# Fused attention and two MoE layers on one core: passes over loads and weights tied behind the newest tile, v's constant columns set once, first blocks later with a buffer of their own

## The chip, the cores and the metric

The kernel runs on one core of a Trainium2 chip. The metric is the device time of one execution in microseconds; the figure that counts is the median of several runs. The engines are named as the profile names them: PE (TensorE, matmuls; PEld its weight loads), DVE (VectorE), ACT (ScalarE), POOL (GpSimd), and SP (SyncE), whose queue issues every DMA of this kernel. Each engine works through its own queue in order; an instruction whose inputs are late holds up all that stand behind it on that engine.

## The reference

Attention over pairs of averaged queries, and then two feed-forward layers one after the other:

```python
def _attn_ref(q, k, v):                      # (4, 8, 1152, 64) each
    q_pool = q.reshape(B, H, S // 2, 2, D).mean(axis=3)
    scores = 1.0 / np.sqrt(D) * np.matmul(q_pool, k.transpose(0, 1, 3, 2))
    scores = scores - np.max(scores, axis=-1, keepdims=True)
    attn = np.exp(scores)
    attn = attn / (np.sum(attn, axis=-1, keepdims=True) + 1e-09)
    return np.matmul(attn, v)

x = attn_out.transpose(0, 2, 1, 3).reshape(B * S, H * D)      # 2304 x 512
h = x @ w_in;  x = (h * np.cos(h)) @ w_out                    # layer 1, 512 -> 2048 -> 512
h = x @ w_in2; out = (h * (1.0 / (1.0 + np.exp(-h)))) @ w_out2  # layer 2, the same sizes
```

The weights of both layers come as 64-bit floats and are turned on the chip into scaled pairs of 16-bit floats (a high and a low part). The same pairs carry q, k, v, the probabilities and the layers' inputs, so most products are three matmuls.

## The kernel before, in words

The work of attention goes in 4 batches of 4 pairs of heads. A pair has 9 tiles of 128 pooled queries against all 1152 keys, 144 tiles in all. A tile t takes these steps, each on its own engine:

- scores (PE, L531 and L539) into PSUM (sp), which holds one tile;
- evacuation with the row minimum, in two parts (DVE, L550), and nb, the bias of the exponential (DVE, L555, 128x1);
- exp in place (ACT, L558), then hi, the 16-bit part of the result (ACT, L564, tile hl), then lo, what hi leaves over (POOL, L569, the other half of hl);
- a transposing DMA from hl to hlT (SP, L571), and four tiles later (LAG) the matmuls with v (PE, L582 and L586), whose sums three tiles share (group_end, DVE and ACT).

Each tile needs a slot of sc, hl and hlT; there are 4 of each. Between a tile's steps the main loop calls advance() four times, which takes one step of every generator in the list bg, and share(), which spends credit on units of layer 1. The generators are:

- pair_prep for the next pair: an absmax of each of k (two), q and v (two) (DVE, L126, tile pm), after q's two rows have been added (POOL, L456, stq), then scales, the high and low parts of q, k, v (qn, kn, vt) and two transposing DMAs (qT, kT). The tile vt of v has an extra column of ones and one of zeros behind its 64 columns, by which the probabilities' sums come out of the same matmul; they are set by two memsets (POOL, L484 and L485) for each of 32 tiles vt. When the prep is through, the pair after next is loaded (SP).
- layer1_weight_steps: 16 pieces of 1 MB of layer 1's weights, loaded on SP (wst), then three passes of VectorE over 128x1024 (L203, L207, L211), a tiny matmul (bm) for the scale, two passes of ScalarE (L224, L225) and one of GpSimd (L226).
- block_steps: two blocks of 256 rows for each batch. x_split takes the block's absmax, splits it into xn (ACT and DVE) and transposes it (xT). The tile xn takes one of the 4 slots of hl. Then the block waits X_LAG steps, if it is not of the first batch, and its units are free to go: 16 units of 12 matmuls (h, L667) and 16 of 12 matmuls (y, L722), with the cosine between.

Units are spent at RATE = 2 for each tile from the second batch on; credit that finds no unit piles up, to 4 at most. What is left of layer 1 runs after the last tile, together with the preparation of layer 2's weights and the first blocks of layer 2; then layer 2 alone.

The order on each queue is not written out: a list scheduler takes the instructions in the order in which the code traces them (a priority; "ahead" moves it), and puts one that is ready early by its own estimate ahead of others that are not. Two means bind it. pin, which is tc.keep_in_program_order, puts an instruction behind everything traced so far on its engine; the passes over the weights are pinned. tc.issue_after(ins) puts what it encloses behind one given instruction of the same engine, and leaves the rest free.

## Time and profile before

| | us |
|---|---|
| median of 3 runs (1362.78 to 1373.58) | 1365.25 |
| the profiled execution | 1363.93 |
| its span, first to last instruction | 1362.1 |
| busy: PE / DVE / ACT / POOL | 1139.0 / 1039.7 / 870.9 / 620.3 |
| first nb to the nb of the second, third, fourth batch | 29.7 to 233.7, 438.9, 628.0 |

The span falls into a short start, the 144 tiles with layer 1 beside them from the second batch on, and a second part in which only the layers are left. An engine's busy time over the whole span mixes the two, so it is read by stretches.

### The profile page before, as it was taken

Reading aid. Unit: us, or ns where it says so; the run is one execution under the profiler, and the core shown is the slowest. Engines: PE = TensorE matmul, PEld = TensorE weight load, DVE = VectorE, ACT = ScalarE, POOL = GpSimd, SP = SyncE. Lnnn points to the kernel's source line nnn. Section 1 sums busy time; section 2 is a strip of 40 time slices with the busy share of each in tenths; the row PEclk is TensorE's granted clock in tenths of the full one; section 3 lists DMA queues with packets and bytes.
Section 4 is the critical chain, followed back from the end, with each engine's and each line's share of the span. In section 5 each row is a group of like instructions: output and inputs, shape, how many; then the busy total and the mean of one; then the engine's idle time right before and its main releaser. Section 6 shows DMA issues by size and latency. Waiting matters only on the chain. (4 is left out here: it accounts for less than half of the span.)

```text
span 1362.1 us, 26442 instructions
## 1 busy us (share of the span) xinstructions
PE 1139.0 (84%) x10668; PEld 915.3 (67%) x10668; DVE 1039.7 (76%) x1927; ACT 870.9 (64%) x1061; POOL 620.3 (46%) x352
## 2 busy tenths in 40 slices
PE   2565465788988777889898899989999999999998
PEld 1343243576666556666676678778788888888887
DVE  6898888789876988888898996886757755444483
ACT  3878787778767777877788774544546633433352
POOL 1656675666556466656556562443667400000000
PEclk9667676889998889999899999999899999999999
DMA  9999999988799999988999965423444000000001
GB/s 290 202 212 226 221 231 183 163 168 166 135 204 177 201 199 198 198 151 186 157 202 188 217 129 109 106 81 71 86 91 112 32 25 32 9 16 17 17 32 32
DMA packets 509594, 186.27 MB, mean 137 GB/s; under 512 B 465952, under 2 KB 484384, under 8 KB 509472
## 3 DMA queue, kind: packets, MB, share of 16 engines
q1 hardware_dynamic: 509472, 184.59, 65.8%
q8 instruction: 83, 1.36, 0.4%
q14 instruction: 39, 0.32, 0.1%
HBM read 66.58 MB, written 9.44 MB: 56 GB/s over the span
## 5 line engine op out<-in xcount | busy, mean ns | idle before, releaser
L569 POOL TENSOR_TENSOR hl<-sc,hl 128x1152 f16<-128x1152 f32 x144 | 367.9, 2565 | 201.2 <-ACT hl L564 105.9
L531 PE MATMUL sp<-kT,qT 128*128 128x512 f16 (+1 forms) x768 | 189.4, 366 | 92.7 <-DVE sc L550 70.8
L550 DVE TENSOR_SCALAR_CACHE_REDUCE sc<-sp,psu 128x512 f32<-128x512 f32 (+1 forms) x288 | 228.9, 807 | 49.6 <-PE sp L531 46.2
L667 PEld LDWEIGHTS <-ih 128*128 128x128 f16 x2304 | 225.5, 99 | 42.9 <-issue 12.4
L558 ACT ACTIVATE sc<-sc,nb 128x1152 f32<-128x1152 f32 x144 | 179.8, 1250 | 114.4 <-DVE nb L555 77.8
L582 PE MATMUL pv<-vt,hlT 128*128 128x130 f16 (+1 forms) x1440 | 195.1, 237 | 65.9 <-DMA hlT<-hl 58.3
L582 PEld LDWEIGHTS <-hlT 128*128 128x128 f16 (+1 forms) x1440 | 146.4, 110 | 96.1 <-DMA hlT<-hl 73.4
L667 PE MATMUL h<-ys,ih 128*128 128x256 f16 x1152 | 195.5, 274 | 4.1 <-ACT gs L683 4.1
L667 PE MATMUL h<-xT,ih 128*128 128x256 f16 x1024 | 184.9, 275 | 3.2 <-DMA xT<-xn 3.1
L586 PE MATMUL pv<-vt,hlT 128*128 128x65 f16 (+1 forms) x1440 | 186.3, 207 | 0.0
L531 PEld LDWEIGHTS <-qT 128*128 128x128 f16 x768 | 76.9, 108 | 156.9 <-issue 104.2
L564 ACT ACTIVATE hl<-sc 128x1152 f16<-128x1152 f32 x144 | 164.6, 1153 | 14.5 <-DMA xT<-xn 9.7
L722 PE MATMUL y<-gh,oh 128*128 128x256 f16 x576 | 162.0, 281 | 7.1 <-ACT y L731 7.1
L722 PE MATMUL y<-gl,oh 128*128 128x256 f16 x576 | 161.8, 281 | 2.9 <-POOL gl L711 2.9
L722 PE MATMUL y<-gh,ol 128*128 128x256 f16 x576 | 161.8, 281 | 0.0
L836 PEld LDWEIGHTS <-op 128*128 128x128 f16 x1512 | 147.9, 98 | 18.0 <-issue 0.6
L667 PE MATMUL h<-ys,il 128*128 128x256 f16 x576 | 157.7, 274 | 0.0
L586 PEld LDWEIGHTS <-hlT 128*128 128x128 f16 (+1 forms) x1440 | 143.0, 108 | 15.8 <-issue 6.1
L667 PE MATMUL h<-xT,il 128*128 128x256 f16 x512 | 140.5, 274 | 0.0
L722 PEld LDWEIGHTS <-oh 128*128 128x128 f16 x1152 | 114.8, 102 | 28.1 <-issue 9.4
L711 POOL TENSOR_TENSOR gl<-tt,gh 128x1024 f16<-128x1024 f32 x36 | 92.1, 2559 | 76.4 <-DVE gh L710 71.2
L667 PEld LDWEIGHTS <-il 128*128 128x128 f16 x1152 | 113.7, 99 | 17.8 <-issue 2.9
(310 smaller groups left out, 2039.9 us busy)
## 6 DMA issues: line engine op xcount, KB each, us to landing
wst<-in_moe_w_in_dram SPq DMA_DIRECT2D x16, 1024.0 KB, 5.8
stk<-in_k_dram SPq DMA_DIRECT2D x32, 288.0 KB, 4.0
stv<-in_v_dram SPq DMA_DIRECT2D x32, 288.0 KB, 4.0
stq<-in_q_dram SPq DMA_DIRECT2D x32, 256.0 KB, 3.1
wst<-in_moe_w_out_dram SPq DMA_DIRECT2D x8, 1024.0 KB, 6.2
wst<-in_moe_w_out_dram SPq DMA_DIRECT2D x16, 512.0 KB, 6.0
ydr<-y SPq DMA_DIRECT2D x9, 512.0 KB, 4.3
y32b<-ydr SPq DMA_DIRECT2D x9, 512.0 KB, 3.3
```

The lines of the kernel that those rows point to most:

```text
L531: nc.tensor.matmul(sp[:, o - a:o - a + n], P.qT[e][:, t, :], kT[:, o:o + n], start=(e == 0), stop=(e == 1))
L550: nc.vector.tensor_scalar(out=T.sc[:, a:z], in0=sp, scalar1=T.P.su, scalar2=None, op0=ALU.mult, op1=ALU.min, accum_out=mx[:, x:x + 1],)
L558: nc.scalar.activation(out=T.sc, in_=T.sc, func=AF.Exp, scale=-1.0, bias=nb)
L564: nc.scalar.activation(out=hi, in_=T.sc, func=AF.Copy)
L569: nc.gpsimd.tensor_tensor(out=T.hl[:, 1, :], in0=T.sc, in1=T.hl[:, 0, :], op=ALU.subtract)
L582: nc.tensor.matmul(G.pv[r, T.gi], T.hlT[:, 0, c, r], P.vt[i][:, c], start=(c == 0), stop=(c == KC - 1), skip_group_check=True,)
L586: nc.tensor.matmul(G.pv[r, T.gi, 0], T.hlT[:, 1, c, r], P.vt[i][:, c, 0], start=False, stop=(c == KC - 1), skip_group_check=True,)
L667: nc.tensor.matmul(hp, wt[:, c, f * 128:(f + 1) * 128], xt(c), start=(i == 0), stop=(i == 3 * NC - 1), skip_group_check=True,)
L711: nc.gpsimd.tensor_tensor(out=G.gl, in0=t, in1=gh, op=ALU.subtract)
L722: nc.tensor.matmul(blk.y[:, oc, :], wt[:, f, oc * 128:(oc + 1) * 128], gt[:, f % 4, :], start=(f == 0 and e == 0 and oc % 2 == 0), stop=(f ...
L836: nc.tensor.matmul(bank, t[:, e, c, :], wt[:, c, :], start=start, stop=True, skip_group_check=True)
```

## The change

It has four parts.

1. pin goes. Three kinds of instruction are kept in a list as they are traced (mark): each tile's nb on DVE, its hi on ACT (where ACT makes it) and its lo on POOL. A context, behind(), puts what is traced in it behind the newest nb on DVE, the second-newest hi on ACT and the second-newest lo on POOL. The steps over the weights after the first pieces, and in pair_prep the five absmax and q's sum, are traced in it. pair_prep takes k, then q's sum, then v, then q.
2. The four buffers of vt are made once, and their columns set once, 8 memsets in place of 64.
3. X_LAG becomes 20 steps for the first batch (it was 0 there) and stays 40 for the others. xn gets a buffer of its own while attention runs, up to the last pair.
4. Credit that finds no unit is dropped.

```diff
-X_LAG = 40
+X_LAG = (20, 40)
...
+    AGE = {"dve": 0, "act": 1, "pool": 1}
...
-    pin = tc.keep_in_program_order
+    anchors = {}
+
+    @contextmanager
+    def behind():
+
+        with ExitStack() as s:
+            for kind, a in anchors.items():
+                k = AGE[kind] + 1
+                if len(a) >= k:
+                    s.enter_context(tc.issue_after(a[-k].ins))
+            yield
+
+    def mark(kind, ins):
+        anchors.setdefault(kind, []).append(ins)
...
-            sc = scale_steps(m, pspool(), (s, u), 14, True, True, True, pin)
+            sc = scale_steps(m, pspool(), (s, u), 14, True, True, True)
...
-            pin(nc.scalar.activation(out=hi, in_=t, func=AF.Copy, scale=s))
-            pin(nc.scalar.activation(out=t, in_=t, func=AF.Copy, scale=s))
-            pin(nc.gpsimd.tensor_tensor(out=lo, in0=t, in1=hi, op=ALU.subtract))
+            nc.scalar.activation(out=hi, in_=t, func=AF.Copy, scale=s)
+            nc.scalar.activation(out=t, in_=t, func=AF.Copy, scale=s)
+            nc.gpsimd.tensor_tensor(out=lo, in0=t, in1=hi, op=ALU.subtract)
...
-                g.append(piece_steps(*x, pin))
-            next(g[0])
+                g.append(piece_steps(*x, lambda ins: ins))
+            with behind():
+                next(g[0])
...
+        at.vt = []
+        for i in range(VT_BUFS):
+            vt = at.p.tile([128, KC, 2, D + 1], F16, tag="vt%d" % i, name="vt", bufs=1)
+            nc.gpsimd.memset(vt[:, :, 0, D:D + 1], 1.0)
+            nc.gpsimd.memset(vt[:, :, 1, D:D + 1], 0.0)
+            at.vt.append(vt)
...
-        nc.gpsimd.tensor_tensor(out=qs, in0=qs, in1=P.q[:, :, 1, :], op=ALU.add)
         m = small.tile([128, 5], F32, name="pm", tag="pm")
         for i in range(2):
-            absmax(m[:, 1 + i:2 + i], P.k[i], AX.XY)
-            yield
-        absmax(m[:, 0:1], qs, AX.XY)
+            with behind():
+                absmax(m[:, 1 + i:2 + i], P.k[i], AX.XY)
+            yield
+        with behind():
+            nc.gpsimd.tensor_tensor(out=qs, in0=qs, in1=P.q[:, :, 1, :], op=ALU.add)
+        for i in range(2):
+            with behind():
+                absmax(m[:, 3 + i:4 + i], P.v[i], AX.XY)
+            yield
+        with behind():
+            absmax(m[:, 0:1], qs, AX.XY)
         yield
-        for i in range(2):
-            absmax(m[:, 3 + i:4 + i], P.v[i], AX.XY)
-            yield
...
-            P.vt[i] = vt = at.p.tile([128, KC, 2, D + 1], F16, tag="vt", name="vt", bufs=VT_BUFS)
-            nc.gpsimd.memset(vt[:, :, 0, D:D + 1], 1.0)
-            nc.gpsimd.memset(vt[:, :, 1, D:D + 1], 0.0)
+            P.vt[i] = vt = at.vt[(2 * (P.b * NP + P.j) + i) % VT_BUFS]
...
-        xn = at.p.tile([128, 2, 2, DM], F16, tag="hl", name="xn", bufs=NB_H)
+        if state.xp is None:
+            xn = at.p.tile([128, 2, 2, DM], F16, tag="hl", name="xn", bufs=NB_H)
+        else:
+            xn = state.xp.tile([128, 2, 2, DM], F16, name="xn", bufs=1)
...
-            while state.credit >= 1 and next(units, False):
+            while state.credit >= 1:
+                if not next(units, False):
+                    state.credit = 0.0
+                    return
                 state.credit -= 1
...
-            if b:
-                for _ in range(X_LAG):
-                    yield
+            for _ in range(X_LAG[b > 0]):
+                yield
```

ScalarE's queue where the first two blocks meet the prep of the sixth pair, before (ps__2424 are that pair's scales; sc is exp, hl is hi; exps of two earlier tiles stand ahead of the first row):

```order
L491 ACTIVATE qn<-stq,ps__2424 128x9x64 x2
L446 ACTIVATE kn<-stk,ps__2424 128x9x64 x2
L446 ACTIVATE vt<-stv,ps__2424 128x9x64 x2
L558 ACT_TABLE_LOAD
L558 ACTIVATE sc<-sc,nb 128x1152
L683 ACTIVATE hk<-h,ca 128x512 x2
L558 ACTIVATE sc<-sc,nb 128x1152
L605 ACTIVATE x_2775<-pvs,den 128x64 x2
L702 ACT_TABLE_LOAD
L702 ACTIVATE tt<-tt,halfpi 128x1024
L649 ACTIVATE xn<-x_521,xs 128x1024
L564 ACTIVATE hl<-sc 128x1152 x3
```

The same pair's prep and the same block's xn after the change:

```order
L581 ACTIVATE sc<-sc,nb 128x1152
L514 ACTIVATE qn<-stq,ps__2351 128x9x64 x2
L467 ACTIVATE kn<-stk,ps__2351 128x9x64 x2
L467 ACTIVATE vt<-stv,ps__2351 128x9x64 x2
L587 ACTIVATE hl<-sc 128x1152
L628 ACTIVATE x_2572<-pvs,den 128x64 x2
L581 ACTIVATE sc<-sc,nb 128x1152
L675 ACTIVATE xn<-x_521,xs 128x1024
L709 ACTIVATE hk<-h,ca 128x512
L581 ACTIVATE sc<-sc,nb 128x1152
L709 ACTIVATE hk<-h,ca 128x512
L587 ACTIVATE hl<-sc 128x1152
```

Where three tiles' hi stood in a row behind four tiles' exp, each hi now stands behind its own or the next tile's exp, and the units' evacuations (hk) begin later.

GpSimd's queue around the same place, before (hl is lo, gl the low part of a unit's product, stq q's sum):

```order
L569 TENSOR_TENSOR hl<-sc,hl 128x1152 x3
L711 TENSOR_TENSOR gl<-tt,gh 128x1024
L456 TENSOR_TENSOR stq<-stq 128x9x64
L569 TENSOR_TENSOR hl<-sc,hl 128x1152 x3
L484 MEMSET vt 128x9
L485 MEMSET vt 128x9
```

And after the change:

```order
L592 TENSOR_TENSOR hl<-sc,hl 128x1152 x5
L483 TENSOR_TENSOR stq<-stq 128x9x64
L592 TENSOR_TENSOR hl<-sc,hl 128x1152 x8
L737 TENSOR_TENSOR gl<-tt,gh 128x1024
L592 TENSOR_TENSOR hl<-sc,hl 128x1152
```

The memsets are gone from between the lo passes, and q's sum has moved back among them.

VectorE's queue at the absmax of the same pair, before (pm<-stk, pm<-stv and pm<-stq are the absmax of k, v and q; den and uo belong to other work):

```order
L598 RECIPROCAL den<-den 128x3
L211 SCALAR_TENSOR_TENSOR wt<-wst,wt 128x1024
L93 TENSOR_SCALAR mw<-wm 128x1
L126 TENSOR_REDUCE pm<-stk 128x1
L126 TENSOR_REDUCE pm<-stv 128x1
L550 TENSOR_SCALAR sc,mx<-sp,psu 128x512
L550 TENSOR_SCALAR sc,mx<-sp,psu 128x640
L126 TENSOR_REDUCE pm<-stv 128x1
L111 TENSOR_SCALAR uo_78<-bm 128x1
L126 TENSOR_REDUCE pm<-stk 128x1
L126 TENSOR_REDUCE pm<-stq 128x1
```

And after the change:

```order
L578 TENSOR_SCALAR nb<-mx 128x1
L140 TENSOR_REDUCE pm<-stk 128x1 x2
L573 TENSOR_SCALAR sc,mx<-sp,psu 128x512
L573 TENSOR_SCALAR sc,mx<-sp,psu 128x640
L573 TENSOR_SCALAR sc,mx<-sp,psu 128x512
L578 TENSOR_SCALAR nb<-mx 128x1
L140 TENSOR_REDUCE pm<-stv 128x1
```

The two of k now stand right behind one tile's nb and those of v and q behind later ones, where before all five stood within one tile among the last weight passes.

## Rows read from the trace of the kernel before

**Rows 1.** Windows: the batches, the rest; busy us by engine, PEclk, DMA share, GB/s.

```profile
29.70:233.70 204.00, 115.72 (x945) 75.39 (x945) 178.65 (x395) 165.23 (x183) 129.06 (x64) 0.68 1.02 216
233.70:438.90 205.20, 171.53 (x1716) 131.20 (x1713) 168.65 (x340) 153.84 (x181) 127.44 (x67) 0.94 0.92 170
438.90:628.00 189.10, 154.12 (x1547) 115.78 (x1545) 162.70 (x334) 147.83 (x178) 112.83 (x63) 0.94 0.99 193
628.00:820.00 192.00, 173.80 (x1725) 131.73 (x1724) 171.74 (x329) 148.48 (x175) 112.59 (x58) 0.97 0.91 176
820.00:1362.10 542.10, 519.10 (x4732) 459.00 (x4730) 338.62 (x497) 245.85 (x335) 134.93 (x88) 0.98 0.21 54
```

**Rows 2.** Waits of DVE, 30 to 820 us: total us, times, longest.

```profile
DVE sc L550 <- PE sp L531: 46.2, 31, 4.1
DVE pm L126 <- DMA stk<-in_k_dram: 16.7, 11, 3.5
...
DVE pm L126 <- DMA stv<-in_v_dram: 7.0, 5, 2.3
...
DVE pm L126 <- POOL stq L456: 3.2, 2, 2.5
```

**Rows 3.** Waits of PE, 30 to 820 us.

```profile
PE pv L582 <- DMA hlT<-hl: 58.3, 30, 5.6
```

**Rows 4.** Groups of instructions, whole span, a tile's steps: busy us, mean ns, idle before.

```profile
L569 POOL TENSOR_TENSOR hl<-sc,hl 128x1152 f16<-128x1152 f32 x144 | 367.9, 2565 | 201.2 <-ACT hl L564 105.9 <-issue 45.9 <-DVE sc L550 12.1
...
L558 ACT ACTIVATE sc<-sc,nb 128x1152 f32<-128x1152 f32 x144 | 179.8, 1250 | 114.4 <-DVE nb L555 77.8 <-DVE den L598 11.7 <-DVE pm L468 6.8
...
L564 ACT ACTIVATE hl<-sc 128x1152 f16<-128x1152 f32 x144 | 164.6, 1153 | 14.5 <-DMA xT<-xn 9.7 <-DMA hlT<-hl 3.9
...
L555 DVE TENSOR_SCALAR nb<-mx 128x1 f32<-128x1 f32 x144 | 29.5, 205 | 0.9
```

**Rows 5.** DMA issues: times, median us from issue to landing.

```profile
hlT<-hl SPq DMA_TRANSPOSE x144, 4.9
```

**Rows 6.** Waits of POOL, 30 to 820 us.

```profile
POOL vt L484 <- PE pv L586: 37.3, 13, 12.0
...
POOL stq L456 <- DMA stq<-in_q_dram: 28.1, 6, 11.2
```

**Rows 7.** Groups of instructions: weight passes of layers 1 and 2, memsets.

```profile
L211 DVE SCALAR_TENSOR_TENSOR wt<-wst,wt 128x1024 int32<-128x1024 int32 x16 | 31.4, 1964 | 0.1
...
L207 DVE SCALAR_TENSOR_TENSOR wt<-wt,wst 128x1024 int32<-128x1024 int32 x16 | 28.7, 1794 | 0.2
...
L311 DVE SCALAR_TENSOR_TENSOR wst<-wst 128x1024 int32<-128x1024 int32 x16 | 20.7, 1292 | 0.0
L308 DVE SCALAR_TENSOR_TENSOR wst<-wst,wt 128x1024 int32<-128x1024 int32 x16 | 20.6, 1288 | 0.1
...
L484 POOL MEMSET vt<- 128x9 f16 x32 | 4.2, 139 | 37.6 <-PE pv L586 37.3 <-POOLq L1237 0.3
```

**Rows 8.** Windows in batch 0, columns as in rows 1.

```profile
136.00:170.00 34.00, 15.41 (x135) 10.10 (x133) 29.15 (x76) 26.72 (x32) 20.82 (x11) 0.65 1.11 221
170.00:204.00 34.00, 22.48 (x200) 16.15 (x200) 28.00 (x67) 28.30 (x29) 27.17 (x15) 0.74 1.09 231
```

**Rows 9.** Timeline of ACT: start us, us, instruction, idle before and its releaser.

```profile
255.98 1.24 ACT L558 ACTIVATE sc<-sc,nb 128x1152 f32<-128x1152 f32 x1
...
281.59 3.25 ACT L564 ACTIVATE hl<-sc 128x1152 f16<-128x1152 f32 x3
...
291.81 1.16 ACT L564 ACTIVATE hl<-sc 128x1152 f16<-128x1152 f32 x1 [4.10 <-DMA xT<-xn]
```

**Rows 10.** Timeline of SP's queue.

```profile
683.56 16.57 SPq L571 DMA_TRANSPOSE hlT<-hl  x5
```

**Rows 11.** Timeline of POOL and DVE around 456 us.

```profile
455.76 2.91 POOL L569 TENSOR_TENSOR hl<-sc,hl 128x1152 f16<-128x1152 f32 x1 [0.40 <-ACT hl L564]
...
456.37 2.33 DVE L627 TENSOR_SCALAR ca<-ui,xu 128x8 f32<-128x8 f32 x1
```

More of the change, by code (lines that the diff above doesn't have):

```diff
@@ L554, in tile_exp @@
         nb = small.tile([128, 1], F32, tag="nb", name="nb", bufs=4)
-        nc.vector.tensor_scalar(
+        mark("dve", nc.vector.tensor_scalar(
             out=nb, in0=mx[:, 0:1], scalar1=mx[:, 1:2], scalar2=PSH * math.log(2.0), op0=ALU.min, op1=ALU.add
-        )
+        ))
         nc.scalar.activation(out=T.sc, in_=T.sc, func=AF.Exp, scale=-1.0, bias=nb)
@@ L563, in tile_hi @@
         if on_act:
-            nc.scalar.activation(out=hi, in_=T.sc, func=AF.Copy)
+            mark("act", nc.scalar.activation(out=hi, in_=T.sc, func=AF.Copy))
         else:
@@ L568, in tile_lo @@
     def tile_lo(at, T):
-        nc.gpsimd.tensor_tensor(out=T.hl[:, 1, :], in0=T.sc, in1=T.hl[:, 0, :], op=ALU.subtract)
+        mark("pool", nc.gpsimd.tensor_tensor(out=T.hl[:, 1, :], in0=T.sc, in1=T.hl[:, 0, :], op=ALU.subtract))
         T.hlT = at.p.tile([128, 2, KC, 128], F16, tag="hlT", name="hlT", bufs=NB_T)
@@ L876, in attention_moe_moe_kernel @@
         state = Weights()
-        state.mp = None
+        state.mp = state.xp = None
+        xn_stack = ExitStack()
         state.ng, state.tail = 0, False
@@ L988, in block_done @@
                 state.mp = moe_pools(moe_stack)
+                state.xp = xn_stack.enter_context(tc.tile_pool(name="xn", bufs=1, reuse_waits="tile"))
             xgens[b, i] = block_steps(b, i)
@@ L1047, in attention_moe_moe_kernel @@
                 at.src_stack.close()
+                for i in range(2):
+                    finish(xgens[b - 1, i])
+                xn_stack.close()
+                state.xp = None
                 w2st_stack = ExitStack()
```

## The prediction

> **What bounds the kernel now.** I read the stretches first, then the waits engine by engine, then single places. The span has two parts [rows 1]. From 29.7 to 820 us, the attention stage, no engine is full: VectorE is the fullest with 178.65 + 168.65 + 162.70 + 171.74 = 681.7 of 790.3 us (86%); TensorE and ScalarE stand at 615 (78%), GpSimd at 482 (61%). From 820 us to the end TensorE is busy 519 of 542 us. In the second part the change alters almost nothing: after the last score matmul TensorE's order holds 9,568 instructions where it held 9,560. So the answer lies in the first part, and there in VectorE's 108.6 us of idle time: what shortens it shortens the run, since VectorE's passes are the same ones before and after.
>
> By what it waited for (30 to 820 us) [rows 2], 46.2 us of VectorE's idle time is waiting for scores, 16.7 + 7.0 = 23.7 us waiting for k and v to land ahead of their absmax, 3.2 us for q's sum. Scores come late because TensorE's queue is held up by earlier work: 58.3 us in 30 waits for a transposed probability tile (hlT) [rows 3]. hlT is the end of a chain nb, exp, hi, lo, transpose, whose bare steps take 0.2 + 1.25 + 1.15 + 2.57 + 4.9 = 10.1 us [rows 4, 5] and which has four tiles' time, 4 x 790.3/144 = 22 us, before TensorE asks for it. What eats the other 12 us is queueing: on ScalarE other passes stand between exp and hi, and on GpSimd the queue's head waits, 37.3 us in 13 waits for v's column memsets and 28.1 us in 6 waits for q's sum [rows 6].
>
> **The change part by part.**
>
> *v's columns set once.* 56 of 64 memsets go. At 139 ns [rows 7] that is 7.8 us of GpSimd, which is idle 39% of the stage: nothing by itself. With them go the 37.3 us in which a memset waited for the matmuls that still read that buffer while lo passes stood behind it. The write of v by ScalarE now meets that wait itself; it stands where it stood, up to eight tiles after the memset, and no wait of it shows in the trace; I price it at nothing (bounds 0 and 37.3 us on ScalarE, beside its 175 us of idle time in the stage).
>
> *q's sum tied and moved behind the k passes.* Before, it could stand one tile behind its own load; now in all pairs from the third on at least three tiles lie between. The 28.1 us of GpSimd's blocking should go, and 3.2 us of VectorE's waiting.
>
> *Absmax tied behind the newest nb.* This looks like the cure of the 23.7 us, but the loads move as well. Counted in tiles from the pair's second k load on SyncE's queue to its absmax on VectorE's, pairs 2 to 15: before 4, 4, 4, 4, 4, 4, 4, 4, 3, 3, 3, 4, 4, 3; now 6, 4, 2, 5, 3, 3, 5, 3, 4, 4, 4, 6, 3, 5. The mean rises from 3.7 to 4.1, but five pairs instead of four have three or fewer. I take 0. Bounds: -23.7 us if every such wait goes, and +11 us: one pair two tiles short and four one tile short of four, at 5.5 us a tile (790.3/144), make 33, against the 23.7 that are there now, plus 2 for v.
>
> *Weight pieces freed from the strict order.* Sixteen pieces, the same passes. Before, a piece's ScalarE and GpSimd passes stood behind everything written before them; now behind the second-newest tile's hi and lo, so they may fill the wait for an exp. The last piece's lo moves from the place after the 38th tile to that after the 32nd. I price the move at nothing: what is done earlier in batch 0 is missing later, VectorE stays 88% busy in batch 0, and the DMA engines show a share of 1.09 to 1.11 from 136 to 204 us, the highest of the run [rows 8], so that loads can hardly come earlier. Bounds: -13 us, which is batch 0's 204 us against its 44.1 MB at the best rate seen, 231 GB/s (191 us); and +5 us.
>
> *Work between exp and hi.* Counting ScalarE's passes between a tile's exp and its hi in the two orders, with each kind's mean from the trace, gives 2.7 us a tile before and 2.0 now (by batch 4.8, 2.8, 1.9, 1.5 and 4.5, 1.0, 1.4, 1.1). Together with GpSimd's freed (37.3 + 28.1)/144 = 0.45 us, the chain to hlT shortens by about 1.2 us a tile. The 30 waits for hlT have a mean of 1.9 us; 1.2 off each, less for the short ones, is about 30 us of TensorE's waiting. VectorE feels a part of that: it waits 46.2 us for scores where TensorE idles 175 us in the stage, 0.26. So **-8 us**; bounds 0 and -30.
>
> *First blocks later, own input buffer.* In the old order the first blocks are split and their units begin right after the last weights, beside the next pair's prep. An exp that starts at 255.98 us waits for its hi until 281.59 us, and two later ones with it, since 21 other passes, the block's xn the last of them, stand between on ScalarE; the hi after these waits another 4.10 us for a transposed xn that holds its buffer [rows 9]. In the new order xn has its own buffer, at most six passes stand between an exp and its hi there, and the first two blocks' units, which began at the 43rd tile's scores and whose last four began at the 60th, run from the 45th to the 66th. Batch 1's VectorE idle time is 205.2 - 168.65 = 36.6 us, that of batches 2 and 3 26.4 and 20.3, a mean of 23.3 [rows 1]; the excess of 13 us is this place's. I take **-10 us**; bounds 0 and -13. What it costs: the units start later, but two blocks hold 64 units and a batch of 36 tiles asks for 72, so the supply and not the start sets how many are done by the end; counted in the order, 8 of TensorE's instructions more (four matmuls) remain after the last score, at 0.28 us at most a matmul, so at most 1.1 us, and overlapped as they are **+0.4 us**. Credit that no longer piles up shifts at most four units once, which the order has already shown in that count.
>
> Sum: -8 - 10 + 0.4 = -17.6 us. The profiled execution took 1363.93 us (1.8 more than its span), so 1346.3; it lies 1.3 under the median of the three runs, and I put the median at **1347**.
>
> **The rivals.**
>
> *DMA or VectorE takes what is given (no change).* For it: share 0.91 to 1.02 over all four batches [rows 1], SyncE issues transposes back to back, five in 16.57 us [rows 10]. Against: 149 MB over the stage would take 646 us at 231 GB/s. If only q's 3 us and a part of the rest come through, 1358 to 1366, say 1362. That the ties leave VectorE's order as it was in effect would give the same time.
>
> *Slower: tied passes wait longer.* An absmax is now fixed behind an nb, and ahead of the scores' evacuation that follows it, so that a late load stops the tile. Pair 4's second k load stands only two tiles ahead. Worked out above, this costs +11 us. Its second half: kT stands four tiles ahead of its first score, now only three for pairs 5 and 13, 5.5 us each, +11. With none of the gains that is 1363.9 + 22 = 1386. It decides if a load takes more than three tile times (16 us) from its place in the queue to landing.
>
> *The shared port takes it back.* A GpSimd pass and a VectorE pass get in each other's way here: a 128x8 pass took 2.33 us beside a lo that started 0.6 us earlier [rows 11]. The two weight passes of two inputs average 1794 and 1964 ns where lo passes run all the time, against 1288 and 1292 for the like-shaped passes of layer 2 [rows 7]: (0.51 + 0.67) x 16 = 18.9 us in batch 0. If GpSimd, no longer blocked, meets twice as many of them, another 19 us are lost: 1347 + 19 = 1366. The Trainium skill, SBUF — State Buffer, "Who interferes with whom", says that the later of two such instructions "fully blocks" until the first is done; by that rule, which the 2.33 us fit, a freed GpSimd queue would give nothing back where VectorE is the bound.
>
> *Twice the gain.* If the smoother start of layer 1 and shorter chain take away half of VectorE's 108.6 us, 1364 - 54 = 1310.
>
> **How the numbers follow.** Forecast 0.45, no change 0.26, slower 0.12, port 0.05, twice the gain 0.12. A measurement of this kernel tells about 1% (13.7 us) from no change. The forecast's own spread, with the bounds of the absmax (-24, +11) and the weights (-13, +5), is about 1330 to 1362; some fifth of it lies above 1351.6. Faster by over 1%: 0.45 x 0.8 + 0.12 + 0.02 = 0.50; slower by over 1%: 0.11; the rest 0.39. The range of 8 in 10 takes in no change and the port rival and a part of the two outer ones: 1322 to 1374.
>
> **What the profile after would show.** Right: no wait of GpSimd for v's buffer, few for q; VectorE's idle time in batch 1 near 25 us; waits of TensorE for hlT near 30 us; the first score of batch 2 some 10 to 15 us earlier; from the last score to the end 550 us as before. Wrong if VectorE's waits for k and v grow past 35 us, if the busy time of its weight passes grows, or if the DMA share reaches 1.1 all over batches 1 and 2 with the tile period unchanged.

## The result, and the profile after

The changed kernel takes 1376.54 us (median of 20 runs, 1365.78 to 1386.79), the kernel before 1366.97 us in the runs made beside it (20 runs, 1362.78 to 1373.58). The ratio is 1.0061, 95% interval 1.0044 to 1.0079: slower by 0.6%, where 1347 us, 1.3% faster, had been forecast. The time lies outside the forecast range. The profiled execution of the changed kernel took 1380.47 us, 16.5 more than that of before, where the medians are 9.6 apart; so a single pair of profiles shows a few us more than the change costs.

The page after, first line of its first part. VectorE was busy for 1039.7 us before, and its number of instructions is the same, 1927: the same passes take 33.5 us longer.

```profile
PE 1142.3 (83%) x10668; PEld 915.5 (66%) x10668; DVE 1073.2 (78%) x1927; ACT 870.2 (63%) x1061; POOL 616.8 (45%) x296
```

Windows of the changed kernel, cut as in [rows 1]: the four batches and the rest; columns as there.

```profile
28.60:254.50 225.90, 117.06 (x902) 74.89 (x901) 207.65 (x406) 167.32 (x185) 136.34 (x54) 0.68 0.91 196
254.50:444.60 190.10, 164.58 (x1651) 123.32 (x1649) 169.49 (x334) 150.46 (x179) 118.13 (x48) 0.95 0.97 184
444.60:637.40 192.80, 166.22 (x1625) 123.62 (x1623) 161.19 (x328) 147.07 (x176) 114.83 (x49) 0.93 1.00 190
637.40:833.00 195.60, 168.98 (x1751) 130.19 (x1751) 184.78 (x336) 148.72 (x175) 110.71 (x47) 0.97 0.91 171
833.00:1378.70 545.70, 521.31 (x4738) 461.62 (x4737) 334.28 (x497) 246.95 (x339) 134.82 (x88) 0.98 0.21 53
```

The stage takes 225.9 + 190.1 + 192.8 + 195.6 = 804.4 us, against 790.3. VectorE's idle time in it fell from 108.6 to 81.3 us, more than the whole gain forecast (27.3 against 17.6). Its busy time rose from 681.7 to 723.1 us: +41.4, some of it passes that moved into the stage, since the rest has 4.3 less. The two make the +14.1. By batch: +21.9, -15.1, +3.7, +3.6. So batch 1 gained 15.1 us, where 10, and 13 at most, had been forecast for it from the later blocks, and batch 0 lost more than that. From the last score to the end it is 550.7 us before and 553.1 after; the repeated run of the changed kernel, below, has 547.1, so this part tells nothing.

Waits of VectorE, 28 to 833 us (total us, times, longest): the waits for k and v, 16.7 + 7.0 us in [rows 2], are 5.6 now, and that for q's sum is gone.

```profile
DVE sc L573 <- PE sp L554: 34.9, 40, 3.0
DVE sc L573 <- PE sp L562: 9.4, 5, 3.1
...
DVE pm L140 <- DMA stk<-in_k_dram: 3.8, 3, 2.1
...
DVE pm L140 <- DMA stv<-in_v_dram: 1.8, 1, 1.8
```

Waits of GpSimd in the same stretch: the waits for v's buffer and for q's load of [rows 6], 65.4 us, no longer stand in the list, but the wait of lo for hi, 105.9 us before, is 196.5 now: GpSimd waits no less, but for another engine.

```profile
POOL hl L592 <- ACT hl L587: 196.5, 51, 24.6
POOL hl L592 <- issue: 37.0, 12, 5.2
POOL gl L737 <- DVE gh L736: 28.2, 11, 6.0
```

Waits of TensorE: hlT 49.6 us, where [rows 3] has 58.3, and a single wait of 15.1 us for qT, where the only one for qT before is 6.1. The repeated run has that 15.1 again.

```profile
PE pv L605 <- DMA hlT<-hl: 49.6, 27, 10.9
PE sp L554 <- DMA qT<-qn: 16.4, 2, 15.1
PE sp L554 <- DMA kT<-kn: 5.2, 1, 5.2
```

That wait shows what happens. The timeline of the kernel before, VectorE, pair 3 (pairs counted from 0): the passes that split q and k, at their bare durations.

```profile
152.00 0.81 DVE L492 SCALAR_TENSOR_TENSOR qn<-stq,ps__1397,qn 128x576 f16<-128x576 f32 x1
...
154.32 0.81 DVE L451 SCALAR_TENSOR_TENSOR kn<-stk,ps__1397,kn 128x576 f16<-128x576 f32 x1
...
156.26 0.81 DVE L451 SCALAR_TENSOR_TENSOR kn<-stk,ps__1397,kn 128x576 f16<-128x576 f32 x1
156.98 0.32 DVE L495 COPY qn<-qn 128x576 f16<-128x576 f16 x1
```

The same pair in the timeline of the changed kernel: VectorE, GpSimd beside it, SyncE's queue, and TensorE, which waits for q.

```profile
179.93 2.63 DVE L515 SCALAR_TENSOR_TENSOR qn<-stq,ps__1391,qn 128x576 f16<-128x576 f32 x1
...
182.60 2.80 DVE L472 SCALAR_TENSOR_TENSOR kn<-stk,ps__1391,kn 128x576 f16<-128x576 f32 x1
185.33 3.39 DVE L225 SCALAR_TENSOR_TENSOR wt<-wst,wt 128x1024 int32<-128x1024 int32 x1
188.64 2.67 DVE L472 SCALAR_TENSOR_TENSOR kn<-stk,ps__1391,kn 128x576 f16<-128x576 f32 x1
...
191.30 2.41 DVE L518 COPY qn<-qn 128x576 f16<-128x576 f16 x1
...
181.90 5.74 POOL L592 TENSOR_TENSOR hl<-sc,hl 128x1152 f16<-128x1152 f32 x2
187.60 3.10 POOL L240 TENSOR_TENSOR ol<-wt,oh 128x1024 f16<-128x1024 f32 x1
190.66 2.87 POOL L592 TENSOR_TENSOR hl<-sc,hl 128x1152 f16<-128x1152 f32 x1
...
191.34 3.36 SPq L530 DMA_TRANSPOSE kT<-kn  x1
194.79 2.88 SPq L520 DMA_TRANSPOSE qT<-qn  x1
...
199.69 2.10 PE L554 MATMUL sp<-kT,qT 128*128 128x512 f16 x6 [15.05 <-DMA qT<-qn]
```

From 181.90 to 193.53 us GpSimd runs reading passes back to back, with ends at about 184.8, 187.6, 190.7 and 193.5. VectorE's next four long passes end at 185.40, 188.72, 191.31 and 193.71: each a GpSimd pass's end plus no more than its own bare duration. A split of k lasts 2.80 us instead of 0.81, the copy of q 2.41 instead of 0.32. kT's transpose is issued 0.03 us after the last split of k, and TensorE gets its scores at 199.69.

To measure this over the whole run I took, for each form of VectorE's passes (tiles, operation, shape), the tenth percentile of its durations over the traces of this study as its bare duration, and added up what every pass took above it: **VectorE's excess**. It is 182.0 us before and 213.6 us after, so it holds 31.6 of the 33.5 us; 176.6 and 208.5 us of it lie in passes that run beside a GpSimd pass. 23.2 of the 31.6 lie in batch 0 (34.0 to 57.2). There the 16 splits and copies of k and q (qn and kn) took 17.3 us before, 7.1 of them beside a GpSimd pass, and take 28.0 us now, 23.1 of them beside one: 10.7 us more. The small passes for the pairs' scales (pu, ps) take 6.8 us more, two of the weight passes (L221, L225) 4.1. A pass that waits for GpSimd counts as busy, so a part of the idle time that went may only have changed its name.

### The profile page after: what moved, and what is told of

The parts are those of the page before. It is cut to its first block, busy times and chain, and to the rows that moved or that the text cites. A ratio compares the mean times of both kernels' runs of the same rounds, so it can differ in the third digit from the quotient of the medians.

```text
span 1378.7 us, 26386 instructions
## 1 busy us (share of the span) xinstructions
PE 1142.3 (83%) x10668; PEld 915.5 (66%) x10668; DVE 1073.2 (78%) x1927; ACT 870.2 (63%) x1061; POOL 616.8 (45%) x296
## 5 line engine op out<-in xcount | busy, mean ns | idle before, releaser
L592 POOL TENSOR_TENSOR hl<-sc,hl 128x1152 f16<-128x1152 f32 x144 | 369.1, 2570 | 290.9 <-ACT hl L587 196.5
L554 PE MATMUL sp<-kT,qT 128*128 128x512 f16 (+1 forms) x768 | 194.4, 370 | 112.3 <-DVE sc L573 76.6
L605 PE MATMUL pv<-vt,hlT 128*128 128x130 f16 (+1 forms) x1440 | 195.3, 240 | 62.3 <-DMA hlT<-hl 49.6
L605 PEld LDWEIGHTS <-hlT 128*128 128x128 f16 (+1 forms) x1440 | 148.7, 112 | 92.2 <-DMA hlT<-hl 57.7
L862 PEld LDWEIGHTS <-op 128*128 128x128 f16 x1512 | 147.8, 98 | 18.4 <-issue 0.6
L609 PEld LDWEIGHTS <-hlT 128*128 128x128 f16 (+1 forms) x1440 | 144.5, 109 | 16.6 <-issue 6.9
L693 PEld LDWEIGHTS <-il 128*128 128x128 f16 x1152 | 113.9, 99 | 16.7 <-issue 1.5
```

The lines of the kernel that those rows point to most:

```text
L554: nc.tensor.matmul(sp[:, o - a:o - a + n], P.qT[e][:, t, :], kT[:, o:o + n], start=(e == 0), stop=(e == 1))
L592: mark("pool", nc.gpsimd.tensor_tensor(out=T.hl[:, 1, :], in0=T.sc, in1=T.hl[:, 0, :], op=ALU.subtract))
L605: nc.tensor.matmul(G.pv[r, T.gi], T.hlT[:, 0, c, r], P.vt[i][:, c], start=(c == 0), stop=(c == KC - 1), skip_group_check=True,)
L609: nc.tensor.matmul(G.pv[r, T.gi, 0], T.hlT[:, 1, c, r], P.vt[i][:, c, 0], start=False, stop=(c == KC - 1), skip_group_check=True,)
L693: nc.tensor.matmul(hp, wt[:, c, f * 128:(f + 1) * 128], xt(c), start=(i == 0), stop=(i == 3 * NC - 1), skip_group_check=True,)
L862: nc.tensor.matmul(bank, t[:, e, c, :], wt[:, c, :], start=start, stop=True, skip_group_check=True)
```

## The experiments

Three theories. **Port**: VectorE's passes, longer beside GpSimd's, took the gain; in its first form, a freed GpSimd does so whatever is tied. **Slack**: the tie puts q's and k's splits too late ahead of their first score (by the orders, the slack is 5, 6, 3 and 2 tiles for pairs 1 to 4 before, 1, 1, 0 and 2 now), and the tiles wait for them whatever GpSimd does. **Chain**: what helps or hurts is the length of GpSimd's step in the chain to hlT. Ratios are to the kernel before, run on the same chip, with 95% intervals; excess and batches are those of the one execution profiled.

**Parts undone and parts alone.** e_prep_free: the changed kernel with the preparation as before.

```diff
-        with behind():
-            nc.gpsimd.tensor_tensor(out=qs, in0=qs, in1=P.q[:, :, 1, :], op=ALU.add)
...
+        nc.gpsimd.tensor_tensor(out=qs, in0=qs, in1=P.q[:, :, 1, :], op=ALU.add)
```

> The changed kernel with the prep of the pairs as before: absmax and q's sum neither tied nor reordered, all else changed. Slack theory (the tie puts VectorE's last split of k and q for the next pair only 1, 1 and 0 tiles ahead of that pair's first score in batch 0, where it was 5, 6 and 3, so TensorE waits 15 us for qT): here the order gives 4, 4, 5 tiles, batch 0 comes back from 226 to about 205 us, no wait for qT or kT over 3 us after the start, and the 15 us gained in batch 1 stay: about 1355 us. Port theory (GpSimd's freed passes fall on VectorE's and lengthen them, whoever is tied): VectorE's busy time stays near 1073 us and the time at 1370 to 1380 us.

1364.33 us, 0.9965 (0.9947 to 0.9983); excess 182.3; batch 0 207.2 us. Without the tie the loss is gone, and the excess is that of before. That rules out the port theory's first form. But only 0.35% is gained, where the slack theory named about 1355 us, and the 15 us gained in batch 1 are gone too. Windows, the four batches up to the last score, columns as above:

```profile
30.24:237.41 207.17, 120.36 (x891) 74.34 (x891) 189.38 (x405) 166.93 (x186) 134.01 (x53) 0.65 0.97 207
237.41:445.45 208.04, 174.03 (x1654) 126.97 (x1653) 170.43 (x332) 149.05 (x179) 116.03 (x49) 0.94 0.92 174
445.45:631.26 185.81, 159.78 (x1641) 121.24 (x1639) 160.64 (x336) 146.70 (x175) 117.47 (x49) 0.95 1.02 196
631.26:817.46 186.20, 165.54 (x1656) 125.67 (x1656) 166.13 (x320) 143.69 (x172) 106.48 (x44) 0.95 0.92 173
```

VectorE's idle time in these is 100.6 us. Counted in the same way, from the first nb to the last score, it is 105.4 before and 80.7 in the changed kernel. So without the tie the passes stay as long as they were, but the idle time stays too.

e_prep_only: that part alone in the kernel before.

```diff
-            absmax(m[:, 1 + i:2 + i], P.k[i], AX.XY)
-            yield
+            with behind():
+                absmax(m[:, 1 + i:2 + i], P.k[i], AX.XY)
+            yield
...
```

> The kernel before with only the prep tied and reordered. The order gives slacks of 2, 1, 1, 1 tiles for pairs 1 to 4 (before 5, 6, 3, 2). Slack theory: batch 0 longer by 10 to 20 us with a wait for qT or kT of several us, about 1380 us. Port theory: weights and memsets stand as before, so VectorE's busy time stays near 1040 us and the time near 1367 us.

1366.40 us, 0.9980 (0.9954 to 1.0005); excess 191.2, batch 0 203.1 us. Alone the tie costs nothing, though it leaves pairs 1 to 4 only 2, 1, 1 and 1 tiles of slack. That speaks against slack, and the 9 us more of excess show no cost either.

e_weights_pinned: the changed kernel with the weight pieces back in the strict order.

```diff
-                g.append(piece_steps(*x, lambda ins: ins))
-            with behind():
-                next(g[0])
+                g.append(piece_steps(*x, pin))
+            next(g[0])
...
```

> The changed kernel with the weight pieces pinned as before, the prep tied, and the rest as changed. Slacks 2, 1, 1, 1. Slack theory in its narrow form (only a slack of 0 with freed weight passes between the splits costs): batch 0 at 205 us, 1360 to 1365 us. Port theory: VectorE's busy time in batch 0 back to 185 us or so, since no freed weight passes fall on lo passes: 1362 to 1368 us. If neither, and the loss is the blocks' part (1374 us by itself), 1374 us or more.

1366.11 us, 0.9999 (0.9983 to 1.0015); excess 184.8. Undoing this part, too, takes the loss away, and here batch 1 keeps its gain (188.8 us).

e_weights_only: freed, tied weights alone, the reverse of that diff in the kernel before.

> The kernel before with only the weight pieces freed and tied. Slacks 4, 4, 5, 7, then 0 for pair 5. Slack theory: batch 0 as before or better, 1360 to 1368 us. Port theory: freed weight passes meet more lo passes, VectorE's busy time in batch 0 up by 10 us or more, 1372 us or more.

1369.99 us, 1.0028 (1.0005 to 1.0050); excess 180.1, batch 0 205.7. So the tie and the freed weights raise the excess to that of the changed kernel only together. For freed weights the port theory had named 1372 us or more and 10 us more of busy time in batch 0, slack 1368 at most; neither came.

e_pace1: the changed kernel with the steps of the preparation two advances apart instead of three for pairs 1 to 4. With this pace v of the next pair is written while the last tiles two pairs back still read that buffer (pair 2's from 102.8 us, pair 0's is read until 119.5), so those tiles multiply other values; the amount of work is the same.

```diff
-PREP_PACE = (2, 2)
+PREP_PACE = (1, 2)
```

> The changed kernel with the steps of the prep two advances apart instead of three for pairs 1 to 4, the ties kept. Slacks by the order 4, 2, 2, 2 instead of 1, 1, 0, 2. Slack theory: most of batch 0's loss comes back, 1358 to 1364 us. Port theory: nothing that matters to it moves, about 1376 us.

1374.14 us, 1.0051 (1.0025 to 1.0078). The slack of pairs 1 to 4 is 4, 2, 2 and 2 tiles and the loss stays; so does the excess, 204.9. Batch 0 does come back, to 208.7 us, as slack had it, but batch 1 takes 201.1 instead of 190.1: here lateness moved time from one batch to another and did not add to it.

e_blocks_only: xn's own buffer, the later blocks and the credit's drop alone.

```diff
-X_LAG = 40
+X_LAG = (20, 40)
...
+            xn = state.xp.tile([128, 2, 2, DM], F16, name="xn", bufs=1)
```

> The kernel before with only the blocks' part: own buffer for xn, 20 steps of lag for the first batch, credit dropped. Slacks in batch 0 as before (5, 6, 3). Slack theory, which takes batch 1's 15 us as this part's gain: batch 1 at about 190 us, batch 0 at 204 us, 1352 us in all. Port theory: a denser GpSimd queue gives the gain back on VectorE, 1362 to 1370 us.

1374.11 us, 1.0029 (1.0007 to 1.0051); batch 1 218.9 us, excess 180.7 (profiled in its slowest execution, 1379.82 us). The part that was to bring 10 us in batch 1 brings nothing there by itself. No theory had this: it is above all the ranges, without more excess.

after_again: the changed kernel itself, once more on another chip.

> The changed kernel itself once more, for how far one profiled execution stands for the others: time 1366 to 1387 us. Both theories: VectorE's busy time goes with the time of the execution profiled (1040 us at 1364, 1073 at 1380), a fast one near 1055 us.

1376.95 us, 1.0068 (1.0031 to 1.0104); excess 211.9; TensorE's 15.1 us wait for qT at the same place.

**GpSimd's reading made short.** In s_before and s_after lo is formed on 288 of its 1152 columns and the rest is set to zero: three quarters of lo are left out.

```diff
-        nc.gpsimd.tensor_tensor(out=T.hl[:, 1, :], in0=T.sc, in1=T.hl[:, 0, :], op=ALU.subtract)
+        nc.gpsimd.memset(T.hl[:, 1, 288:S], 0.0)
+        nc.gpsimd.tensor_tensor(out=T.hl[:, 1, 0:288], in0=T.sc[:, 0:288], in1=T.hl[:, 0, 0:288], op=ALU.subtract)
```

> The kernel before with lo computed on the first 288 of 1152 columns alone; the other columns are set to zero by a memset, so they leave lo out. GpSimd's reading passes over the probabilities become a quarter as long. Slacks by the order 5, 6, 2, 4. Port theory (a GpSimd pass that runs beside VectorE's lengthens them): VectorE's busy time falls by 60 us or more, the run by 20 to 60 us. Slack theory: a shorter chain alone, 10 to 20 us.

> The changed kernel with the same cut: lo on 288 of 1152 columns, the others zero. Slacks by the order 2, 1, 0, 1, as short as in the changed kernel. Port theory: with the long GpSimd passes gone nothing is taken back, so it is faster than the kernel before with the same cut, by 10 to 20 us. Slack theory: the scores of pairs 2 and 3 wait for their transposes as before the cut, batch 0 is longer than in the cut kernel before by 10 to 20 us, and the whole run slower than it by 5 us or more.

1340.72 us, 0.9802 (0.9775 to 0.9828), and 1318.47 us, 0.9647 (0.9619 to 0.9675). Excess 91.2 and 92.2. With GpSimd out of the way the change is worth 1340.72 - 1318.47 = 22.2 us, where the sum of the prediction was 17.6. Windows of s_before, the four batches:

```profile
30.24:221.54 191.30, 111.45 (x924) 69.68 (x923) 152.42 (x384) 158.23 (x177) 90.16 (x95) 0.71 1.09 228
221.54:429.91 208.37, 171.59 (x1715) 131.98 (x1716) 154.59 (x352) 157.96 (x185) 91.19 (x105) 0.93 0.91 169
429.91:623.43 193.52, 167.51 (x1593) 123.04 (x1591) 142.42 (x332) 147.73 (x178) 84.84 (x101) 0.89 1.00 191
623.43:794.98 171.55, 160.25 (x1652) 122.65 (x1650) 143.75 (x325) 143.46 (x170) 79.77 (x89) 0.98 1.01 189
```

And of s_after:

```profile
28.30:238.14 209.84, 115.96 (x892) 74.44 (x890) 168.16 (x407) 167.49 (x185) 96.72 (x86) 0.66 1.00 209
238.14:418.79 180.65, 159.53 (x1636) 121.35 (x1636) 147.46 (x331) 150.53 (x178) 82.73 (x84) 0.97 1.05 193
418.79:599.49 180.70, 160.68 (x1640) 121.88 (x1641) 139.70 (x328) 145.31 (x172) 83.11 (x85) 0.93 1.09 201
599.49:770.20 170.71, 160.39 (x1671) 123.87 (x1668) 143.26 (x326) 142.57 (x173) 75.70 (x80) 0.98 1.05 195
```

Batches 1 and 2 are 27.7 and 12.8 us shorter with the change. Batch 0 is 18.5 us longer even so; it holds 407 VectorE passes instead of 384, work that is missing later, and TensorE waits 19.9 us in it for kT and qT instead of 3.9, as slack had it, without a cost to the whole.

n_before and n_after tell port from chain: GpSimd's step is as long as with the whole lo, but it writes for most of it and reads nothing there (three quarters of lo are left out again).

```diff
-        nc.gpsimd.tensor_tensor(out=T.hl[:, 1, :], in0=T.sc, in1=T.hl[:, 0, :], op=ALU.subtract)
+        nc.gpsimd.tensor_tensor(out=T.hl[:, 1, 0:288], in0=T.sc[:, 0:288], in1=T.hl[:, 0, 0:288], op=ALU.subtract)
+        for _ in range(2):
+            nc.gpsimd.memset(T.hl[:, 1, 287:S], 0.0)
```

> The kernel before with lo on 288 columns and two memsets behind it, each 865 columns, so that GpSimd is as long at a tile as before (0.84 + 2 x 0.83 = 2.5 us) and the chain as long, but reads SBUF in a third of that time; the other columns are zero, lo is left out there. Port theory: VectorE's busy time falls as with the short lo (about 950 us), the time to 1340 to 1350 us. Chain theory (the short lo gained because GpSimd's step and queue were shorter): as the kernel before, about 1367 us.

> The changed kernel with the same long but mostly not reading GpSimd step, other columns zero. Slacks by the order 1, 1, 1, 0. Port theory: faster than the kernel before with the same step, by 10 to 20 us, near 1325 us. Chain theory: near the changed kernel's 1376 us and slower than the kernel before with the same step by 5 us or more.

1345.45 us, 0.9829 (0.9780 to 0.9878), and 1320.79 us, 0.9655 (0.9610 to 0.9700): the change is worth 24.7 us. The excess is 98.6 and 112.0 us, 13.4 more with the change, and the gain comes all the same: excess is not lost time one for one. Groups of GpSimd in n_after:

```profile
L594 POOL MEMSET hl<- 128x865 f16 x288 | 240.2, 839 | 13.2
L592 POOL TENSOR_TENSOR hl<-sc,hl 128x288 f16<-128x288 f32 x144 | 123.6, 859 | 257.7 <-ACT hl L587 257.3
```

2 x 839 + 859 = 2537 ns a tile, against 2570 ns for the whole lo. A step of the old length that reads little is as good as a short one, so the length of GpSimd's step is not it. The chain theory falls.

s_prep_free: s_after with the preparation as before (the diffs of s_after and e_prep_free together).

> The changed kernel with the preparation as before (q's sum, the five maxima and their order untied) and lo formed on 288 of the 1152 columns only, the rest set to zero; three quarters of lo are left out. Compare with s_after, 1318.5 us. If the tie costs through GpSimd's passes alone, nothing of its cost is left here: 1314 to 1325 us, batch 0 208 us or more. If the tie costs also because q and k are late for TensorE, batch 0 gets shorter than 205 us and the time is 1300 to 1313 us. If the tie is a gain by itself once GpSimd is out of the way (it takes away GpSimd's wait for q), the time is 1326 us or more.

1315.26 us, 0.9639 (0.9600 to 0.9679), against 0.9647 with the tie; batch 0 202.8 us. With the short lo the tie neither costs nor gains, where with the whole lo undoing it is worth 12.2 us. What it costs goes through GpSimd's passes; as a cost to the whole run by lateness alone, slack falls. In batch 0 the lateness is there, as the sign named for it says (below 205 us, 7.0 less than with the tie), but the later batches make up for it. GpSimd's waits for q's load are back here (25.5 us in 10 waits) and cost nothing.

**The same work in shorter reading passes.** lo in two passes of 576 columns; nothing is left out.

```diff
-        nc.gpsimd.tensor_tensor(out=T.hl[:, 1, :], in0=T.sc, in1=T.hl[:, 0, :], op=ALU.subtract)
+        for o in range(0, S, S // 2):
+            z = slice(o, o + S // 2)
+            last = nc.gpsimd.tensor_tensor(out=T.hl[:, 1, z], in0=T.sc[:, z], in1=T.hl[:, 0, z], op=ALU.subtract)
```

> The changed kernel with lo in two passes of 576 columns; nothing is left out. Port theory: a VectorE pass that meets a lo waits for half a pass at most, so VectorE's busy time falls by some 30 us and the time by 10 to 15 us, to 1362 to 1366 us, if GpSimd's second instruction (about 0.3 us a tile, from 0.84 us for 288 columns and 2.57 for 1152) is hidden. Chain theory: 0.3 us more a tile on the chain, 1376 to 1380 us.

1350.25 us, 0.9863 (0.9804 to 0.9922), 12 us below the port theory's range; excess 152.7. Two groups of h_after: half a lo takes 1470 ns, so both take 14% more of GpSimd's time than the whole, yet the weight pass that averaged 2330 ns takes 1719.

```profile
L594 POOL TENSOR_TENSOR hl<-sc,hl 128x576 f16<-128x576 f32 x288 | 416.8, 1470 | 252.9 <-issue 158.0
...
L225 DVE SCALAR_TENSOR_TENSOR wt<-wst,wt 128x1024 int32<-128x1024 int32 x16 | 27.5, 1719 | 0.0
```

> The kernel before with lo in two passes of 576 columns each; nothing is left out. If the split gains by itself, since VectorE's waiting passes get in between the halves, it is worth on this kernel what it was worth on the changed one, about 26 us: 1338 to 1352 us, and h_after (1350.3 us) has then no gain of the change in it. If the split only lets the change's gain through, this kernel stays within 1360 to 1372 us. In between (1353 to 1359 us) both are in it.

1362.38 us, 0.9984 (0.9961 to 1.0008), though the excess falls from 182.0 to 149.0 there too. Waits of GpSimd and VectorE in h_before, 30 to 825 us:

```profile
POOL stq L456 <- DMA stq<-in_q_dram: 57.8, 12, 11.5
POOL vt L484 <- PE pv L588: 20.4, 8, 5.0
...
DVE pm L126 <- DMA stk<-in_k_dram: 38.5, 17, 10.0
```

VectorE's freed time went into waits: for k's loads 38.5 us instead of 16.7, while GpSimd waits 78.2 us for q's load and v's buffer. In h_after GpSimd has none of these two waits, and VectorE waits 19.8 us for k. So the split is no gain by itself; it lets the change's gain through. That the waits are why it is none by itself is read from these lines, not tried.

h_prep_free: h_after with the preparation as before.

> The changed kernel with the preparation as before and lo in two passes of 576 columns; nothing is left out. If the tie still costs with the split lo, 1332 to 1345 us, below h_after's 1350.3 by the 12 us that undoing the tie gave with lo whole. If the split has taken away what the tie cost, 1346 to 1355 us, the same as h_after. If the tie is a gain once the split has shortened GpSimd's passes, 1356 us or more.

1345.14 us, 0.9853 (0.9809 to 0.9897); excess 145.8. By the ratios it is the same as h_after within the intervals: with shorter reading passes no cost of the tie is to be seen. These two are faster than both kernels, by 1.4 to 1.5% against the one before.

**What the tie leaves unexplained.** v's columns, weights and blocks together, without the preparation's tie, against the same kernel without them: 0.4% faster with the whole lo (e_prep_free against the kernel before), 1.3% with lo in halves (h_prep_free against h_before), 1.7% with the short lo (s_prep_free against s_before). The excess hardly differs within a pair: 182.3 and 182.0, 145.8 and 149.0, 85.2 and 91.2. VectorE's idle time from the first nb to the last score falls by 4.8, 18.4 and 18.6 us. So with the lo passes whole most of the parts' gain is missing, though they take no more of VectorE's time than before. By what way was not found.

**Which part brings the 22 us.** Each part alone in s_before, by the diffs above; for v's columns:

```diff
-            P.vt[i] = vt = at.p.tile([128, KC, 2, D + 1], F16, tag="vt", name="vt", bufs=VT_BUFS)
-            nc.gpsimd.memset(vt[:, :, 0, D:D + 1], 1.0)
-            nc.gpsimd.memset(vt[:, :, 1, D:D + 1], 0.0)
+            P.vt[i] = vt = at.vt[(2 * (P.b * NP + P.j) + i) % VT_BUFS]
```

> The kernel before with the short lo and with v's columns set once, alone. The prediction priced it at nothing by itself: 1338 to 1344 us, as s_before. If the waits of GpSimd for v's buffer held up the tiles, 1325 to 1337 us.

> The kernel before with the short lo and with the weight pieces freed from the strict order and tied behind the newest tile's steps, alone. By the prediction's term for the work between exp and hi, of which this part brings most, 4 to 8 us less than s_before's 1340.7: 1332 to 1337 us. If it moves work to and fro at no gain, 1338 to 1344 us; if it costs by lateness, without GpSimd's passes, above 1344 us.

> The kernel before with the short lo (288 of 1152 columns, the rest zero; three quarters of lo are left out) and with the later blocks and xn's own buffer alone. Compare with s_before, 1340.7 us. By the prediction's term, 10 us less and all of it in batch 1: 1327 to 1334 us, batch 1 below 200 us against 208. If the gain of batch 1 comes only together with the other parts, 1337 to 1344 us and batch 1 at 205 us or more.

1342.47, 1346.01 and 1350.32 us; 0.9824 (0.9784 to 0.9863), 0.9853 (0.9788 to 0.9918) and 0.9864 (0.9817 to 0.9912), against s_before's 0.9802. None gains alone; the last two are above the ranges named for no gain, though their intervals overlap that of s_before. Freed weights move work into batch 0 (206.4 us instead of 191.3) and out of batches 1 and 2 (198.4 and 188.1 instead of 208.4 and 193.5), with nothing left over; the later blocks take batch 1 to 201.4 us, but batch 3 and the rest come out 7.2 and 6.6 us longer, the latter no more than the 6 us by which the rest differs between two executions of the changed kernel. All three together are s_prep_free, 0.9639. The gain belongs to a combination; which of them it needs was not tried.

## Why the prediction was wrong

**The step that failed** is in its first paragraph: "what shortens [VectorE's idle time] shortens the run, since VectorE's passes are the same ones before and after". The idle time did shrink, by 27.3 us. The passes are the same in number and kind, but not in length: the excess grew by 31.6 us. The sum had terms for where passes wait and none for how long they last beside GpSimd. Of the 1.9% between the forecast (1.3% faster) and the result (0.6% slower), this step accounts for 1.0: undoing the tie alone brings the excess back to 182.3 us and the time from 1.0061 to 0.9965.

**A second step failed beside it**: the terms of -8 and -10 us. In e_prep_free, where the passes are no longer than before, the kernel gains 4.8 us by the medians in place of 17.6, VectorE's idle time falls from 105.4 to 100.6 us and batch 1 takes 208.0 us. The same parts gain 1.3 and 1.7% where lo is cut in two or shortened, so what holds them back is GpSimd's long passes again; the way is open.

**The port rival** had that mechanism, at 19 us and a chance of 0.05. The price was of the right order (31.6 us of excess measured, 12.2 of time), the trigger and the passes were not. It priced the weight passes, which hold 4.1 of the 23.2 us of batch 0. And it took a GpSimd freed from blocking to be what makes passes meet; e_weights_pinned, where GpSimd waits no more for v's buffer and 2.3 us for q's load, has an excess of 184.8. What makes them meet is the order: with the preparation tied behind the newest tile's steps and the weights too, q's and k's splits come while GpSimd works through its lo passes and the weights' own. I had counted where kT's transpose stands on SyncE's queue, and not where the splits that feed it stand on VectorE's. How the two ties together bring this about was read from the orders and from pair 3, not tried pass by pass.

By the sentence of the Trainium skill (SBUF — State Buffer, "Who interferes with whom") that the later of two such instructions "fully blocks", a VectorE pass should begin its work when GpSimd's pass ends, and so end no more than its bare duration later; the timeline at 180 to 194 us shows that. The conclusion drawn from it, nothing gained where VectorE is the bound, was nearer to the result than the forecast.

**The terms.** *The sum, -17.6*: where GpSimd reads little, the change brings 22.2 and 24.7 us (s, n), so the total was about right there, but by luck, since its parts were not. *Work between exp and hi, -8, and blocks later, -10*: put in alone, the weights and the blocks bring nothing, with the whole lo (1.0028, 1.0029) or the short one; the gain of batch 1, 15.1 us, is one of parts together, with the whole lo of the tie too, and batch 0 pays for it. TensorE's waits for hlT fell by 8.7 us, not by 30. *v's columns, 0*: as forecast when alone (with the short lo). *q's sum*: the 28.1 us of blocking went, and s_prep_free, which has 25.5 us of it again, is no slower than s_after; so there they are worth nothing. *Absmax tied, 0 (-24 to +11)*: the waits for k and v fell by 18.1 us, near the good end, while VectorE's passes grew by more. *Weights freed, 0 (-13 to +5)*: within the bounds by itself, 0.3% slower, and one half of the tie's loss. *Blocks' cost, +0.4*: from the last score to the end 550.7 us before, 553.1 and 547.1 in two executions after; too small to be seen.

**The other rivals.** The slower one (a late load stops the tied absmax) did not happen: those waits are 5.6 us. Its second half, q and k too late for the scores, is there once, 15.1 us for qT at pair 3, but through the splits and not through the queue. Of the signs named as right, GpSimd's waits went and VectorE's idle time in batch 1 is 20.6 us, where about 25 was forecast; but the waits for hlT are 49.6 us and not near 30, and batch 2's first nb comes at 444.6 us instead of 438.9, later and not earlier. Of those named against it, a growing busy time of the weight passes came in part: 31.4 us in [rows 7] to 37.3 us for one kind of layer 1, though the other fell from 28.7 to 26.9. Groups of VectorE in the changed kernel:

```profile
L225 DVE SCALAR_TENSOR_TENSOR wt<-wst,wt 128x1024 int32<-128x1024 int32 x16 | 37.3, 2330 | 0.0
L221 DVE SCALAR_TENSOR_TENSOR wt<-wt,wst 128x1024 int32<-128x1024 int32 x16 | 26.9, 1683 | 0.3
...
L518 DVE COPY qn<-qn 128x576 f16<-128x576 f16 x16 | 13.2, 823 | 0.1
```

The last row, q's copy, was 5.6 us (347 ns each) before.

**What stays open**: why the three parts gain so little with the whole lo even without the tie; why weights or blocks alone cost 0.3% with no more excess; which combination of v's columns, weights and blocks brings the 22 us; and how much of the 11.5 us by which batch 0 is longer in s_prep_free than in s_before (202.8 and 191.3) is the 24 VectorE passes that moved into it.

## What to carry to other kernels

When a change only reorders work, the durations of the passes are part of what it changes: look in the profile for forms whose mean lies well above their shortest, find the engine that runs beside them, and ask of the new order which passes will now meet it. A tie that fixes a pass behind a step of the newest tile also fixes what it runs beside. Where a long reading pass of GpSimd cannot be moved, cutting it in two, though it costs GpSimd 14% more time here, can let a reordering's gain through: here neither gives much by itself (0.9984 and 0.9965), and both together 0.9853.

## What the runs showed of the hardware

VectorE loses a good part of its time to GpSimd's passes here: 176.6 of its 1039.7 busy us are excess of passes beside GpSimd's before, 84.1 with the short lo. Not all kinds of passes are hit. Mean durations in ns in the changed kernel, of the passes that overlap a GpSimd pass by 0.05 us at most and of those that do by more, with their counts (my count over the trace):

```
                                        alone        beside GpSimd
absmax of k, 128x576                    744 (10)     742 (22)
scores' evacuation with max, 128x512    740 (59)     740 (85)
nb, 128x1                               203 (64)     204 (80)
split of k, two inputs, 128x576         807 (21)     2047 (11)
weights L221, two inputs, 128x1024      1219 (7)     2044 (9)
cast gh, 128x1024                       679 (24)     1823 (12)
copy of q, 128x576                      317 (11)     1938 (5)
scale constants, 128x3 (pu)             164 (11)     2245 (5)
```

The absmaxes and the evacuations are indifferent to GpSimd; the splits, casts, copies and even the 128x3 constants are not, and wait out GpSimd's pass. In batch 0 the change brings the wrong ones beside GpSimd: of the absmaxes' time 11.7 of 14.1 us lay beside GpSimd before and 7.5 of 14.8 after, of q's and k's splits and copies 7.1 of 17.3 and then 23.1 of 28.0 us. The section of the Trainium skill named above draws the line in the same place (reductions and forms that write out an accumulator stay clear, two inputs from SBUF or a copy do not), and says that a GpSimd pass which only writes leaves two-input passes alone. The n kernels agree: the two-input pass L225 takes 1443 ns in n_after and 1490 in s_after, against 2330 with the whole lo, while the excess as a whole is 112.0 in n_after and 92.2 in s_after (98.6 in n_before, 91.2 in s_before).
